# Attention into a mixture of experts on one core: products of zeros among the first heads, their stages skewed by one, and a third weight slot

## The chip, the cores and the metric

One core of a Trainium2 chip (trn2). The metric is device time in microseconds (us) of one execution, lower is better. The profile is of one such execution. Engines by the profile's names: PE (TensorE: matrix products and transposes, PEld its weight loads), DVE (VectorE), ACT (ScalarE), POOL (GpSimd), SP (the queue that issues all DMAs).

## The reference

```python
B, H, S, D = 4, 8, 576, 64          # attention
N, DM, E, FF = 2304, 512, 4, 1024   # experts, N = B * S
scores = q @ k^T / sqrt(D)
cum    = cumsum(log(clip(f, 1e-4, 1)))
scores = where(causal, -1e9, scores + cum_i - cum_j)
attn   = exp(scores - max) ; attn /= sum(attn) + 1e-9
x      = (attn @ v) with the heads side by side        # (2304, 512)
p      = probs / (sum(probs) + 1e-9)
out    = sum over e of p[:, e] * (relu(x @ w1[e]) @ w2[e])
```

All in float32.

## The kernel before, in words

**Tiles.** The tokens lie in 9 chunks of 256. A *job* is one batch, a pair of heads and a part of its queries (the first 256 or the other 320); a *head* in this text is one head of a job. Heads 0 to 7 (jobs 0 to 3, `FIRST = 8`) make the rows of chunk 0. A product of float32 operands is made of several in a reduced format: each operand is split into a high part (an ACT copy) and a low part (a subtraction on DVE or POOL).

**A head of the startup.** `prep_hi` copies the high part of q and k on ACT (`hi`, L297) and casts q on POOL (`q`, L298); `prep_lo` makes the low parts on POOL (`kl` L306, `hi` L312; on DVE for job 0). `qk_pe` makes the scores on PE (L350, four products), `qk_min` adds the mask and takes the maximum on DVE (L364), `qk_exp` is the exponential on ACT (L379, two tiles), `tr_pe` transposes on PE (L445, three), `tr_hi` (ACT, L455) and `tr_lo` (DVE, L462) split the transposed tile, `av_both` makes six products with v on PE (L493). After two heads `recip` (DVE L395 and L398, then POOL L400) and `spread` (a PE transpose L410 and an ACT copy L416) give the divisor, and `fin` multiplies on DVE (`xs`, L556) and splits into `xh` (ACT, L565) and `xl` (DVE, L568). `prep_v` splits v of a job (POOL L273, DVE L274). `late_sums` makes the second part of the running sums on DVE (L161) and sends them through DRAM for the later heads.

**Experts.** A *step* takes two weights (128 x 1024 each, the slices of w1 and w2 for 128 hidden units) for one chunk. Its first layer is `l1_k` (L698, 24 products of 256 columns: k = 0 to 3 is the pair of heads, so k needs `xh` of job k), then `gate` (ACT L709, DVE L710), then the second layer (L728, 12 products of 512 columns). `w_load` fetches a weight (512 KB) into a `wr` slot (SP, L644). `w_split` makes `wh` on ACT (L653) and `wl` in two halves (L657), on DVE for even weights below 16 and on POOL for all others. A `wr` slot is free when its split has ended. The first 8 steps use 16 weights once each.

**Order.** `startup()` writes the order of each engine by hand, stage by stage: in stage s head s has its exponential, head s+1 its scores, head s+2 its `prep`, head s-2 its products with v. Each engine runs its list in order. After it, a planner lays the steps and the heads from 8 on (`head_steps`, each with a due place through `pace`) on the engines. In that part PE always has first-layer and second-layer products in its list between those of the heads.

Of the kernel before, what the change touches and what calls it, by code (L numbers as in the profile page):

```python
# [29 lines left out]
DIRECT = (0, 1, 2, 3, 4)  # L30
LEAD = 3
W_DVE = tuple(range(0, 16, 2))
W_SLOT = (4, 5)
NEAR = 2
LATE = 6
L1_SLOT = {8: (0, 1), 9: (2,), 10: (3,)}
JOBS = ((0, 0), (1, 0), (2, 0), (3, 0), (0, 1), (1, 1), (2, 1), (3, 1))


# [32 lines left out]
def fused(ctx: ExitStack, tc: tile.TileContext, qk, v, f, probs, w, out):  # L72
# [13 lines left out]
    xh_p = SB("xh", 4)  # L86
    xf_p = SB("xf", 4)
    w_p = SB("w", 6)
    wr_p = SB("wr", 2)
    g_p = SB("g", 2)  # L90
    acc_p = SB("acc", 4)
    dr_p = ctx.enter_context(tc.tile_pool(name="dr", bufs=4, space=bass.MemoryType.DRAM))
# [20 lines left out]
    def decays():  # L113
        nc.sync.dma_start(out=fr, in_=f)
        first_loads()
        for t in q2:
            nc.gpsimd.memset(t[64:66, :].bitcast(F32), 8.0)
        make_identity(nc, ident)
        for t in [zero] + v4:
            nc.gpsimd.memset(t.bitcast(F32), 0.0)  # L120
        nc.vector.memset(ones, 1.0)
        for c in PARTS:
            nc.vector.tensor_scalar(
                out=fr[:, c], in0=fr[:, c], scalar1=1e-4, scalar2=1.0, op0=ALU.max, op1=ALU.min
            )
            nc.scalar.activation(out=fr[:, c], in_=fr[:, c], func=AF.Ln)
        nc.scalar.activation(out=warm, in_=ones[:, :1], func=AF.Exp)
        sums(0)
        nc.gpsimd.memset(mask, 0.0)
        nc.gpsimd.affine_select(  # L130
            out=mask[:, S - 128 :],
            in_=mask[:, S - 128 :],
            pattern=[[-1, 128]],
            compare_op=ALU.is_ge,
            fill=NEG,
            base=0,
            channel_multiplier=1,
        )
        for h in range(NEAR):
            jobs[0].near(h)  # L140
        for n in range(2):
            nc.sync.dma_start(out=ncd[:, n, :CH], in_=nc2[n][:, :CH].bitcast(F32))
        first_raw(2)
        for j in (0, 2):
            n = 1 if j == 0 else 0
            nc.sync.dma_start(
                out=first_kl[j // 2][64:66, 512 * n :].bitcast(F32).rearrange(
                    "p (h s) -> p h s", s=CH
                ),
                in_=ncd[2 * (j + n) : 2 * (j + 2), :, :CH].rearrange("h n s -> n h s"),  # L150
            )
        first_raw(3)
        w_load(0)
        w_load(1)
        nc.sync.dma_start(out=pr_r, in_=probs)
        jobs[NPR].load()

# [65 lines left out]
    class Job:  # L223
# [76 lines left out]
        def prep_lo(self, hh):  # L300
            if hh not in self.kl:
                self.rows(hh)
            wq, wk, ko, qo = self.wq, self.wk, self.ko, self.qo
            r, hi, kl = self.raw[:, hh, :], self.hi[hh], self.kl[hh]
            eng = nc.gpsimd if self.half == 0 and self is not jobs[0] else nc.vector
            eng.tensor_tensor(  # L306
                out=kl[:64, :wk],
                in0=r[:64, ko : ko + wk],
                in1=hi[:64, ko : ko + wk].bitcast(F32),
                op=ALU.subtract,  # L310
            )
            eng.tensor_tensor(  # L312
                out=hi[64:128, qo : qo + wq],
                in0=r[64:128, qo : qo + wq],
                in1=hi[64:128, qo : qo + wq].bitcast(F32),
                op=ALU.subtract,
            )

# [224 lines left out]
        def av(self, hh):  # L543
            self.av_pe(hh)
            self.av_top(hh)
            self.av_add(hh)

        def fin(self):
            w_ = self.wq
            pieces = place(self.b, self.half)  # L550
            k = self.pr
            direct = any(p[1] in DIRECT for p in pieces)
            if self not in jobs[:NPR]:
                self.spread()
            if direct:
                nc.vector.tensor_tensor(  # L556
                    out=self.xs[:, :w_],
                    in0=self.o[:, :w_] if self in jobs[:NPR] else self.xs[:, :w_],
                    in1=self.r[:, :w_],
                    op=ALU.mult,  # L560
                )
# [79 lines left out]
    def w_load(n):  # L641
        if n < NW and n not in wraw:
            wraw[n] = wr_p.tile([128, 1024], F32, tag="wr", name=f"wr{n}")
            nc.sync.dma_start(out=wraw[n], in_=w[n % 32])  # L644

    def w_split(n):
        if n >= NW:
            return
        w_load(n)
        wh[n] = w_p.tile([128, 1024], F32R, tag="wh", name=f"wh{n}")  # L650
        wl[n] = w_p.tile([128, 1024], F32R, tag="wl", name=f"wl{n}")
        r = wraw.pop(n)
        nc.scalar.activation(out=wh[n], in_=r, func=AF.Copy)  # L653
        for a in (0, 512):
            z = a + 512
            eng = nc.vector if n in W_DVE else nc.gpsimd
            eng.tensor_tensor(  # L657
                out=wl[n][:, a:z], in0=r[:, a:z], in1=wh[n][:, a:z].bitcast(F32), op=ALU.subtract
            )
        w_load(n + 1)  # L660
        w_load(n + 2)

    acc = {}
    l2 = {}
# [140 lines left out]
    def pace(n):  # L805
# [8 lines left out]
            m += 1  # L814
        upto(m)

    def startup():

        J = lambda h: heads[h] if 0 <= h < FIRST else (None, None)
# [4 lines left out]
        heads[0][0].prep_v()  # L824
        for h in range(2):
            J(h)[0].begin(h)
        heads[0][0].qk_pe(0, (0, 1))
        heads[0][0].qk_min(0, 0)
        heads[0][0].qk_min(0, 1)
        for s in range(FIRST + 3):  # L830
            (j, hh), (m, mm), (n, nn), (i, ii) = J(s), J(s + 1), J(s + 2), J(s - 2)
            if n:
                n.begin(nn)
                n.prep_hi(nn)
                n.prep_lo(nn)
            if m:
                m.qk_pe(mm, m.its)
                for t in m.its:
                    m.qk_min(mm, t)
            if j:  # L840
                for t in j.its:
                    j.qk_exp(hh, t)
            if i:
                i.av_both(ii)
            if j:
                j.tr_pe(hh, 0)
                j.tr_hi(hh, 0)
                j.tr_lo(hh, 0)
                if hh == 1:
                    j.recip()  # L850
                if hh == 0 and s > 0:
                    j.prep_v()
            if s >= 2 and s % 2 == 0 and s <= FIRST:
                heads[s - 1][0].spread()
            if s >= 4 and s % 2 == 0:
                heads[s - 4][0].fin()
            if s == LATE:
                late_sums()
            if s in W_SLOT:
                w_split(W_SLOT.index(s))  # L860
            for k in L1_SLOT.get(s, ()):
                if k == 0:
                    steps[0].l1_zero()
                for fi in range(2):
                    steps[0].l1_k(fi, k)
        j = heads[FIRST][0]
        w_split(2)
        j.prep(0)
        w_split(3)
        j.prep_v()  # L870
        j.begin(0)
        normalize()
# [1 line left out]
            w_split(n)  # L874

    pt0 = [pt_p.tile([128, 1216], F32R, tag=x, name=f"{x}_first") for x in ("pth", "ptl")]
    with tc.manual_schedule():
        startup()
    prev = None
# [66 lines left out]
```

## Time and profile before

| | |
|---|---|
| median of 3 runs | 1033.07 us (1031.91 to 1033.54) |
| the profiled execution | 1033.34 us, of which 1031.6 us are the span from the first to the last instruction |
| PE busy | 1003.7 us (97%) |
| DVE, ACT, POOL busy | 535.8, 447.5, 326.9 us |
| the chain that ended last | PE 88%, DMA 3%, DVE 3%, ACT 1%, POOL 1% |

How to read it: the chain is followed back from the last instruction to what released each one. The busy share of PE is counted in time, so a product that runs at half clock counts double; the granted clock has its own line.

### The profile page before, as it was taken

What the parts mean: (1) busy time and instruction counts of PE and PEld (TensorE: products, weight loads), DVE (VectorE), ACT (ScalarE), POOL (GpSimd) and SP (SyncE); (2) the same over time, 40 slices, a digit from 0 to 9 for tenths busy, and PEclk for the clock granted to TensorE, in tenths of its full rate; (3) what the DMA queues carried; (4) which work ended last, traced back from release to release, by engine and by line L of the source; (5) the groups of instructions that cost most, each with busy time, mean ns of one, the idle gap of its engine ahead of it and who ended that gap; (6) DMA issues with size and microseconds to landing.
All of it is one profiled execution on the core that took longest, in us unless ns stands there. A gap on an engine that the chain in (4) does not pass through costs nothing.

```text
span 1031.6 us, 16826 instructions
## 1 busy us (share of the span) xinstructions
PE 1003.7 (97%) x6561; PEld 917.3 (89%) x6561; DVE 535.8 (52%) x1181; ACT 447.5 (43%) x897; POOL 326.9 (32%) x357
## 2 busy tenths in 40 slices
PE   4789999999999999999999999999999999999998
PEld 4679899989999999999999999999999999999997
DVE  5667655686867756667566665532222222222222
ACT  5466765566656536455455455422121211212110
POOL 6466876251402204031223144213030311303010
PEclk9699999999999999999999999999999999999999
DMA  5255653342412314022131332211120202102001
GB/s 175 62 183 170 179 151 112 95 160 90 131 50 81 101 49 131 15 91 97 58 123 55 111 118 61 86 59 44 40 82 1 83 19 64 51 32 82 1 21 62
DMA packets 30544, 87.02 MB, mean 84 GB/s; under 512 B 3301, under 2 KB 5537, under 8 KB 30465
## 3 DMA queue, kind: packets, MB, share of 16 engines
q1 hardware_dynamic: 30464, 85.94, 26.5%
q8 instruction: 52, 0.85, 0.3%
q14 instruction: 28, 0.22, 0.1%
HBM read 81.06 MB, written 4.87 MB: 83 GB/s over the span
## 4 chain that ended last, share of the span: by engine, by line
PE 88%; DMA 3%; DVE 3%; ACT 1%; POOL 1%; issue 1%; SPq 0%; ACTq 0%; DVEq 0%; POOLq 0%
PE l L698 37%; PE l L728 36%; PE s L350 5%; PE t L445 5%; PE o L514 4%; DMA wr<-in_w 2%; DMA raw<-in_qk 1%; DVE wl L657 1%; ACT wh L653 1%; PE b L410 1%; POOL wl L657 0%; DVE v L285 0%; DVE hi L312 0%; POOL hi L312 0%; DVE xs L556 0%
## 5 line engine op out<-in xcount | busy, mean ns | idle before, releaser
L657 POOL TENSOR_TENSOR wl<-wr,wh 128x512 fp32r<-128x512 f32 x176 | 228.2, 1325 | 351.9 <-ACT wh L653 348.1
L698 PE MATMUL l<-xh,wh 128*128 128x256 f32 x1152 | 330.6, 287 | 3.1 <-ACT wh L653 3.0
L698 PE MATMUL l<-xh,wl 128*128 128x256 f32 x1152 | 327.9, 285 | 0.7 <-DVE wl L657 0.6
L698 PE MATMUL l<-xl,wh 128*128 128x256 f32 x1152 | 327.9, 285 | 0.1
L710 DVE SCALAR_TENSOR_TENSOR gl<-l,gh 128x512 fp32r<-128x512 f32 x144 | 99.1, 689 | 271.5 <-ACT gh L709 270.7
L728 PE MATMUL l<-wh,gh 128*128 128x512 f32 x576 | 231.1, 401 | 0.0
L698 PEld LDWEIGHTS l<-xh,wh 128*128 128x128 f32 x1152 | 220.8, 192 | 9.2 <-ACT wh L653 4.2
L728 PE MATMUL l<-wl,gh 128*128 128x512 f32 x576 | 227.5, 395 | 0.0
L698 PEld LDWEIGHTS l<-xl,wh 128*128 128x128 f32 x1152 | 220.7, 192 | 5.6 <-DVE xl L568 0.3
L728 PE MATMUL l<-wh,gl 128*128 128x512 f32 x576 | 225.5, 394 | 0.0
L698 PEld LDWEIGHTS l<-xh,wl 128*128 128x128 f32 x1152 | 220.6, 192 | 2.0 <-DVE wl L657 1.1
L709 ACT ACTIVATE gh<-l 128x512 fp32r<-128x512 f32 x144 | 85.5, 595 | 278.5 <-PE l L698 277.5
L379 ACT ACTIVATE p<-p,nm 128x576 f32<-128x576 f32 (+2 forms) x160 | 96.0, 601 | 92.1 <-DVE nm L364 91.7
L653 ACT ACTIVATE wh<-wr 128x1024 fp32r<-128x1024 f32 x96 | 100.0, 1054 | 68.1 <-DMA wr<-in_w 44.7
L728 PEld LDWEIGHTS l<-wh,gl 128*128 128x128 f32 x576 | 108.3, 188 | 23.0 <-DVE gl L710 0.4
L728 PEld LDWEIGHTS l<-wh,gh 128*128 128x128 f32 x576 | 109.1, 189 | 16.2 <-ACT gh L709 0.4
L728 PEld LDWEIGHTS l<-wl,gh 128*128 128x128 f32 x576 | 109.1, 189 | 15.5
L750 DVE SCALAR_TENSOR_TENSOR acc<-l,prob,acc 128x512 f32<-128x512 f32 x126 | 93.9, 748 | 28.8 <-PE l L728 26.1
L364 DVE CUSTOM_DVE_ANT_0 p<-s,mask 128x288 f32<-128x288 f32 (+2 forms) x160 | 75.9, 478 | 52.4 <-PE s L350 51.4
L298 POOL CAST q<-raw 64x320 fp32r<-64x320 f32 (+1 forms) x56 | 27.7, 496 | 226.7 <-PE s L350 208.9
L462 DVE TENSOR_TENSOR ptl<-t,pth 128x320 fp32r<-128x320 f32 (+2 forms) x120 | 65.9, 553 | 63.2 <-ACT pth L455 62.7
L445 PE MATMUL t<-ident,p 128*128 128x128 f32 x480 | 81.5, 279 | 4.0 <-ACT p L379 3.5
(80 smaller groups left out, 1001.5 us busy)
## 6 DMA issues: line engine op xcount, KB each, us to landing
wr<-in_w SPq DMA_DIRECT2D x96, 512.0 KB
raw<-in_qk SPq DMA_DIRECT2D x16, 896.0 KB
raw<-in_qk SPq DMA_DIRECT2D x12, 512.0 KB
vr<-in_v SPq DMA_DIRECT2D x16, 320.0 KB
out<-acc SPq DMA_DIRECT2D x16, 256.0 KB
first<-in_qk SPq DMA_DIRECT2D x4, 512.0 KB
vr<-in_v SPq DMA_DIRECT2D x12, 128.0 KB
first<-in_v SPq DMA_DIRECT2D x1, 512.0 KB
```

Source lines behind the costliest of these rows:

```text
L350: nc.tensor.matmul(out=ps[:, at : at + z - a], lhsT=lhsT, rhs=rhs, start=(m == 0), stop=(m == 1),)
L364: nc.vector.tensor_tensor_reduce(out=pt[:, a:z], in0=ps, in1=mask[:, m0 + a : m0 + z], scale=-0.125, scalar=BIG if n == 0 else nm[:, col : ...
L379: nc.scalar.activation(out=pt[:, :w_], in_=pt[:, :w_], func=AF.Exp, scale=-1.0, bias=self.nmax[hh][:, c : c + 1], accum_out=self.ssum[:, h ...
L445: nc.tensor.transpose(ps[:, at : at + 128], self.p[hh, it][:, TOK0[jt] : TOK0[jt] + 128], ident)
L462: nc.vector.tensor_tensor(out=lo[:, a0 + first : a0 + at - first], in0=ps[:, 2 * first : at], in1=hi[:, a0 + first : a0 + at - first].bitc ...
L653: nc.scalar.activation(out=wh[n], in_=r, func=AF.Copy)
L657: eng.tensor_tensor(out=wl[n][:, a:z], in0=r[:, a:z], in1=wh[n][:, a:z].bitcast(F32), op=ALU.subtract)
L698: nc.tensor.matmul(out=self.l1p[:, fi, :], lhsT=lhsT, rhs=rhs[:, k, :], start=(k == 0 and m == 0 and not self.whole), stop=(k == 3 and m = ...
L709: nc.scalar.activation(out=self.gh, in_=self.l1p, func=AF.Relu)
L710: nc.vector.scalar_tensor_tensor(out=self.gl, in0=self.l1p, scalar=0.0, in1=self.gh.bitcast(F32), op0=ALU.max, op1=ALU.subtract,)
L728: nc.tensor.matmul(out=l2[tt], lhsT=lhsT, rhs=rhs, start=(self.ps == 0 and fi == 0 and m == 0), stop=(self.ps == 1 and fi == 1 and m == 2),)
L750: nc.vector.scalar_tensor_tensor(out=acc[c][:, tt, :], in0=l2[tt], scalar=sc, in1=acc[c][:, tt, :], op0=ALU.mult, op1=ALU.add,)
```

## The change

- `idle_pe(n)` issues n products of the tile `zero` (128 x 128 by 128 x 512) into a PSUM tile that nobody reads: 8 before the first scores, one ahead of the transposes and one behind them in each stage with a head, 3 in each stage from 7 on (33 in all).
- The stages are skewed: `av_both` of a head stands one stage after its exponential (before: two), so there are 10 stages and not 11. The scores stand behind the last products with v of the stage before; the exponential stands ahead of the `prep` on ACT. `fin` of a job is cut in three calls (`fin_mult`, `fin_hi`, `fin_lo`) that stand in the odd stages from 3 on, two heads after the exponential of the job's second head. `prep_v` moves to the odd stages, behind `recip`.
- `prep_lo` makes the low part of q first, that of k second.
- Weight 0 is still split in stage 4, weight 1 in stage 6 (before: 5). `late_sums` moves from stage 6 to stage 8, with the split of weight 2 behind it (before: after the last stage). The split of weight 3 goes ahead of the `prep` of head 8.
- Step 0's first layer moves to stages 7 to 9 (before: 8 to 10).
- `wr` has three slots; weight 2 is fetched at the start, and a split of weight n fetches up to weight n+3.

```diff
-W_SLOT = (4, 5)
+W_SLOT = (4, 6)
-LATE = 6
-L1_SLOT = {8: (0, 1), 9: (2,), 10: (3,)}
+L1_SLOT = {7: (0, 1), 8: (2,), 9: (3,)}
-    wr_p = SB("wr", 2)
+    wr_p = SB("wr", 3)
             eng.tensor_tensor(
+                out=hi[64:128, qo : qo + wq],
...
+            )
+            eng.tensor_tensor(
                 out=kl[:64, :wk],
...
+        def fin_mult(self):
+            w_ = self.wq
+            nc.vector.tensor_tensor(
+                out=self.xs[:, :w_], in0=self.o[:, :w_], in1=self.r[:, :w_], op=ALU.mult
+            )
+        def fin_hi(self):
+            th, _ = x_tiles(self.b)
+            nc.scalar.activation(out=th[:, self.pr, :], in_=self.xs[:, :CH], func=AF.Copy)
+        def fin_lo(self):
+            th, tl = x_tiles(self.b)
+            nc.vector.tensor_tensor(
+                out=tl[:, self.pr, :],
+                in0=self.xs[:, :CH],
+                in1=th[:, self.pr, :].bitcast(F32),
+                op=ALU.subtract,
+            )
...
         w_load(1)
+        w_load(2)
...
+        w_load(n + 3)
...
+    def idle_pe(n):
+        for _ in range(n):
+            nc.tensor.matmul(out=idle_ps, lhsT=zero[:, :128], rhs=zero, start=True, stop=True)
+        idle_pe(8)
         heads[0][0].qk_pe(0, (0, 1))
...
-        for s in range(FIRST + 3):
+        for s in range(FIRST + 2):
+            (i, ii), (j, hh), (m, mm), (n, nn) = J(s - 1), J(s), J(s + 1), J(s + 2)
+            ends = s % 2 == 1
+            if ends and s >= 3:
+                heads[s - 2][0].fin_mult()
+            if j:
+                for t in j.its:
+                    j.qk_exp(hh, t)
+            if ends and s >= 3:
+                heads[s - 2][0].fin_hi()
             if n:
                 n.begin(nn)
-                n.prep_hi(nn)
-                n.prep_lo(nn)
+                n.prep(nn)
             if m:
                 m.qk_pe(mm, m.its)
                 for t in m.its:
                     m.qk_min(mm, t)
+            if ends and s >= 3:
+                heads[s - 2][0].fin_lo()
             if j:
+                idle_pe(1)
+                j.tr_pe(hh, 0)
+                idle_pe(1)
+                j.tr_hi(hh, 0)
+                j.tr_lo(hh, 0)
             if i:
                 i.av_both(ii)
+            if ends and j:
+                j.recip()
+                if m:
+                    m.prep_v()
+            if not ends and s >= 2:
+                i.spread()
             if s in W_SLOT:
                 w_split(W_SLOT.index(s))
+            if s >= FIRST - 1:
+                idle_pe(3)
             for k in L1_SLOT.get(s, ()):
...
+            if s == FIRST:
+                late_sums()
+                w_split(2)
         j = heads[FIRST][0]
-        w_split(2)
+        w_split(3)
         j.prep(0)
-        w_split(3)
         j.prep_v()
```

## Rows read from the trace of the kernel before

**Rows 1.** The page's span in 40 slices: busy tenths of PE, and the granted clock of PE in tenths.

```profile
PE   4789999999999999999999999999999999999998
PEclk9699999999999999999999999999999999999999
```

**Rows 2.** Busy time of the engines by stretch: the stretch in us, its length, PE busy (count), PEld, DVE, ACT, POOL, then the granted clock of PE, the DMA share and GB/s.

```profile
35.50:39.00 3.50, 1.41 (x9) 1.08 (x9) 2.82 (x8) 1.78 (x6) 0.33 (x2) 0.99 0.50 150
39.00:45.50 6.50, 5.15 (x23) 5.06 (x24) 1.79 (x7) 0.69 (x2) 0.74 (x2) 0.50 0.06 14
47.30:60.00 12.70, 12.53 (x80) 10.86 (x79) 10.44 (x26) 9.18 (x22) 9.00 (x10) 1.00 0.58 187
60.00:70.00 10.00, 9.28 (x60) 7.84 (x59) 6.34 (x13) 5.93 (x12) 7.00 (x9) 1.00 0.52 158
70.00:80.00 10.00, 7.66 (x46) 6.90 (x45) 7.46 (x19) 7.31 (x19) 6.77 (x9) 0.83 0.50 159
100.00:110.00 10.00, 9.38 (x62) 8.24 (x61) 6.52 (x18) 7.55 (x19) 9.43 (x10) 1.00 0.56 158
200.00:400.00 200.00, 199.50 (x1350) 184.14 (x1349) 146.94 (x342) 117.61 (x239) 53.29 (x59) 1.00 0.29 94
```

**Rows 3.** What PE waited for in the whole span: total us, times, longest us.

```profile
PE t L445 <- ACT p L379: 3.5, 3, 1.9
PE s L350 <- POOL hi L312: 3.3, 4, 1.1
PE l L698 <- ACT wh L653: 3.0, 2, 2.3
PE s L350 <- DMA kl<-ncd: 1.7, 1, 1.7
PE b L410 <- POOL rb L400: 1.4, 1, 1.4
PE o L514 <- DVE ptl L462: 0.6, 1, 0.6
PE l L698 <- DVE wl L657: 0.6, 1, 0.6
```

**Rows 4.** The longest wait of any engine between 45 and 130 us: total us, times, longest us.

```profile
ACT wh L653 <- DMA wr<-in_w: 12.9, 10, 2.9
```

**Rows 5.** Pieces of the chain that ended last, between 46 and 75 us: start, length, what.

```profile
46.01 1.05 ACT wh L653
...
49.00 3.63 DMA wr<-in_w
...
55.10 5.26 DMA wr<-in_w
...
73.67 1.06 ACT wh L653
74.78 0.50 PE l L698 x2
```

**Rows 6.** Instructions of ACT in the startup, in order of time: start, length, what, in brackets the idle time before it and its releaser. 17.07 is the exponential of head 2, 19.91 of head 3, 36.87 of head 7; 41.13 is the divisor's copy of job 3, 45.69 the `xh` of job 3.

```profile
17.07 0.39 ACT L379 ACTIVATE p<-p,nm 128x128 f32<-128x128 f32 x1
...
19.91 0.40 ACT L379 ACTIVATE p<-p,nm 128x128 f32<-128x128 f32 x1
...
28.21 0.61 ACT L297 ACTIVATE hi<-first 128x512 fp32r<-128x512 f32 x1
28.73 0.39 ACT L379 ACTIVATE p<-p,nm 128x128 f32<-128x128 f32 x1
...
36.54 0.42 ACT L565 ACTIVATE xh<-xs 128x256 fp32r<-128x256 f32 x1 [1.81 <-DVE xs L556]
36.87 0.39 ACT L379 ACTIVATE p<-p,nm 128x128 f32<-128x128 f32 x1
...
38.42 0.49 ACT L455 ACTIVATE pth_first<-t 128x384 fp32r<-128x384 f32 x1 [0.59 <-PE t L445]
41.13 0.38 ACT L416 ACTIVATE r<-b 128x256 f32<-128x256 f32 x1 [2.22 <-PE b L410]
...
45.69 0.42 ACT L565 ACTIVATE xh<-xs 128x256 fp32r<-128x256 f32 x1 [3.87 <-DVE xs L556]
```

**Rows 7.** Products on PE in the startup, as above. The first waits for rows of `kl` from DRAM; the next two have one shape; 40.69 is the only product of zeros of the kernel before; 47.20 is the last of step 0's first layer.

```profile
14.47 0.47 PE L350 MATMUL s<-kl,q 66*128 66x128 f32 x1 [1.67 <-DMA kl<-ncd]
...
16.77 0.41 PE L493 MATMUL o<-pth_first,v 128*128 128x256 f32 x1
...
20.52 0.28 PE L493 MATMUL o<-pth_first,v 128*128 128x256 f32 x1
...
40.69 0.78 PE L681 MATMUL l<-zero 128*128 128x512 f32 x1
...
47.20 0.28 PE L698 MATMUL l<-xh,wl 128*128 128x256 f32 x1
```

**Rows 8.** The low parts of a weight on DVE (two pairs) and on POOL (weight 3), and the low part of head 8's k on POOL, as above.

```profile
28.33 1.84 DVE L657 TENSOR_TENSOR wl<-wr,wh 128x512 fp32r<-128x512 f32 x2 [0.52 <-ACT wh L653]
...
47.66 0.73 POOL L306 TENSOR_TENSOR kl<-raw,hi 64x256 fp32r<-64x256 f32 x1 [7.02 <-ACT hi L297]
...
49.61 2.68 POOL L657 TENSOR_TENSOR wl<-wr,wh 128x512 fp32r<-128x512 f32 x2
...
53.75 1.29 DVE L657 TENSOR_TENSOR wl<-wr,wh 128x512 fp32r<-128x512 f32 x2 [0.68 <-ACT wh L653]
```

More of the change, by code (lines that the diff above doesn't have):

```diff
@@ L306, in prep_lo @@
             eng.tensor_tensor(
+                out=hi[64:128, qo : qo + wq],
+                in0=r[64:128, qo : qo + wq],
+                in1=hi[64:128, qo : qo + wq].bitcast(F32),
+                op=ALU.subtract,
+            )
+            eng.tensor_tensor(
                 out=kl[:64, :wk],
@@ L309, in prep_lo @@
                 in1=hi[:64, ko : ko + wk].bitcast(F32),
[L310 to L315, printed above, removed]
                 op=ALU.subtract,
@@ L546, in av @@
             self.av_add(hh)
+        def fin_mult(self):
[12 more added lines that the diff above has]
+                in1=th[:, self.pr, :].bitcast(F32),
+                op=ALU.subtract,
+            )
         def fin(self):
@@ L552, in fin @@
             direct = any(p[1] in DIRECT for p in pieces)
-            if self not in jobs[:NPR]:
-                self.spread()
+            self.spread()
             if direct:
@@ L557, in fin @@
                     out=self.xs[:, :w_],
-                    in0=self.o[:, :w_] if self in jobs[:NPR] else self.xs[:, :w_],
+                    in0=self.xs[:, :w_],
                     in1=self.r[:, :w_],
@@ L829, in startup @@
         heads[0][0].qk_min(0, 1)
-        for s in range(FIRST + 3):
-            (j, hh), (m, mm), (n, nn), (i, ii) = J(s), J(s + 1), J(s + 2), J(s - 2)
+        for s in range(FIRST + 2):
[8 more added lines that the diff above has]
+                heads[s - 2][0].fin_hi()
             if n:
                 n.begin(nn)
-                n.prep_hi(nn)
-                n.prep_lo(nn)
+                n.prep(nn)
             if m:
@@ L839, in startup @@
                     m.qk_min(mm, t)
+            if ends and s >= 3:
+                heads[s - 2][0].fin_lo()
             if j:
-                for t in j.its:
-                    j.qk_exp(hh, t)
+                idle_pe(1)
[3 more added lines that the diff above has]
+                j.tr_lo(hh, 0)
             if i:
                 i.av_both(ii)
[L845 to L858, printed above, removed]
+            if ends and j:
[4 more added lines that the diff above has]
+                i.spread()
             if s in W_SLOT:
                 w_split(W_SLOT.index(s))
+            if s >= FIRST - 1:
+                idle_pe(3)
             for k in L1_SLOT.get(s, ()):
@@ L876, in fused @@
     pt0 = [pt_p.tile([128, 1216], F32R, tag=x, name=f"{x}_first") for x in ("pth", "ptl")]
+    idle_ps = ps_1.tile([128, 512], F32, tag="l1", name="idle")
     with tc.manual_schedule():
```

## The prediction

> **What bounds the kernel now.** I read the slices first: PE is full from about 47 us on and its clock sags only in the second slice [rows 1]. Then the stretches: from 200 us on PE is busy 99.8% at full clock [rows 2], and neither the products nor their order there are changed. What can move is what PE loses before. Its waits name it [rows 3]: in the startup the exponentials, POOL's low parts, the rows of `kl` from DRAM and POOL's divisor; after it the high and low parts of weights. Next to the waits stands the clock: it was at half from 39 to 45.5, after a stretch in which PE had worked 1.41 of 3.5 us [rows 2]. Before 25 us the clock column reads 1.00, but a product of 256 columns lasted 0.41 us at 16.77 and 0.28 at 20.52 [rows 7], so I take the clock there from durations: half at first, full from between these two. Last the chain: between 46 and 75 us it goes from a split to the transfer into its slot, to the next split, to PE [rows 5], and ACT waited 12.9 us for weights in 10 waits [rows 4]. Two pieces therefore set the end: when step 0's first layer is through (47.20 + 0.12 = 47.3 us [rows 7]; I call this X) and what PE loses behind it.
>
> **The weights: third slot.** The even weights 2 to 10, five of them, began their splits at 46.01 and, the last, at 73.67 [rows 5]: 27.7 us for four pairs, 6.9 us a pair with two slots. One round of a slot is a transfer of 3.6 to 5.3 us [rows 5], ACT's 1.05 and 1.3 us of DVE or 2.7 of POOL [rows 8], so a pair costs 6.0 to 9.0. With three slots the same round carries three weights: 4.6 us a pair. PE needs for a step 24 x 256 + 12 x 512 columns, 5.1 us at 2.4 GHz, and the heads' products come on top. So weights stop being last. What was lost to them: 3.0 + 0.6 us of PE's waits [rows 3], and the half clock after the longest (2.3 us): 0.17 of the 10 us from 70 to 80 [rows 2], 1.7 us. Sum 5.3. The waits of 0.6 for `ptl` stay. The first weights come in time too: weight 4 is asked for when POOL ends with weight 1, near 38.5, and lands by 42.5 to 44 (before: 52.6, the end of the transfer from 49.00). Bounds: 3.6 if the clock sags all the same, 5.9 if the 0.6 for `ptl` goes as well.
>
> **The stages up to the exponential of head 7 (before: 36.87 [rows 6]).** Head 2's scores wait for DRAM rows until 14.47 [rows 7], a transfer that is not moved, so its exponential stays at about 16.9. After that I add up what follows what. Exponential to the high part of the transposed tile is 36.87 to 38.42, 1.55 us [rows 6]. In an even stage PE then has a zero product (512 columns: 0.21 us at 2.4 GHz, 0.43 at 1.2), six products with v (1152 columns, 0.48 or 0.96) and the divisor's transposes (0.2 or 0.4, 0.3 until ACT sees them), and ACT's copy (0.3) stands ahead of the next exponential: 3.05 us at full clock, 4.2 at half. An odd stage is ACT's own work: exponentials 0.9, `xh` 0.42, `hi` 0.61, high part 0.49 [rows 6], 2.15 with the overlaps. Stages 4 and 6 carry a weight's high part on ACT (0.95 to the next start). In stage 5 `fin_mult` stands on DVE behind weight 0's low parts, 1.84 us [rows 8], and ACT's `xh` and head 7's `hi` behind it: 1.5 more. So head 3 at 16.9 + 3.7 = 20.6 (before 19.91), head 4 at 22.75, 5 at 26.75, 6 at 30.4, 7 at 34.4 with full clock, 36.7 with half in stages 4 and 6. I take 35.6: 1.3 us won. The skew itself wins a stage; the zeros and the copy ahead of the exponential give most of it back. The cover of the zeros is the wait for exponentials; where it is gone they cost 16 x 0.21 or 16 x 0.43, and this is the difference of the bounds. The eight at the start run from 2.5 us on, done by 6, before the first scores at 8.8: nothing.
>
> **From there to X.** Exponential to high part 1.55; then on PE a zero product, head 6 with v, three zeros, step 0's zero product, 12 first-layer products, head 7 with v, the transposes: 3.9 us at full clock, 7.4 at half. The divisor's copy thus starts 5.3 to 9.0 after the exponential; I take 7.2, since the clock was half in this place before [rows 2]: 42.8 (before 41.13 [rows 6]). Now weight 2's split stands ahead of the last `fin`: on ACT 0.3 + 1.05, on DVE 1.3 to 1.84 (`fin_mult` is queued behind it, and `late_sums` has ended by then), then `xs` 0.41, `xh` 0.42 and 0.25 of hand-overs: 3.9. Six products with the wait for `xl`: 1.1. X is 47.8, 0.5 later than before. PE waits some 2.0 us in this place (42.8 + three zeros, six products, three zeros = 44.7, against 46.7). Waits of 1.9 and 2.3 us were followed by half clock [rows 2, 3, 5], shorter ones of 1.1 were not always; half a chance of the 1.7 us seen at 70 to 80 is 0.9. Startup: 1.4 us lost. Bounds: 2.8 won (full clock all through, X = 44.5) to 4.2 + 1.7 lost (half clock all through, X = 51.5).
>
> The low parts of a pair on DVE lasted 1.84 us beside POOL's subtractions and 1.29 elsewhere [rows 8]. The Trainium skill (SBUF — State Buffer, Summary: rules for kernel authors) says that of a DVE instruction with two SBUF inputs and a GpSimd one that reads SBUF the second to issue blocks until the first has ended; by that the pair in stage 4 would cost 1.29 + 2 x 0.73 = 2.75, as an estimate, and the sum would be 0.9 higher. The row shows a delay of this kind but smaller, and the sum uses the row.
>
> **The sum.** 1033.34 + 1.4 - 5.3 = 1029.4; the profiled execution stands 0.27 above the median, so I write 1029.4 for the median too. Under 0.2% (2.1 us) a measurement of this kernel hardly tells from no change.
>
> **Rivals.** (a) The zeros hold the clock at full through the startup: X = 44.5 and no sag behind it, 1033.3 - 2.8 - 5.3 = 1025.2. For it: the zeros fill part of the waits that stood between PE's bursts. Against it: stages 4 to 6 still hold waits for DVE and POOL of over 1 us, and stage 9 one of 2. The Trainium skill (TensorE: Matmul & The Clock Gate, Why this matters for your kernels) advises dense work to leave half clock and no idle gaps to stay out of it; that rule would give this case, and the drop after 39 us agrees with its second half.
> (b) The zeros run at half clock and PE sets the stages: X = 51.5, the sag behind it, 1033.3 + 5.9 - 5.3 = 1033.9, no change. For it: half clock from 39 to 45.5 under continuous work. Against it: the same work brought the clock back at 45.5.
> (c) Slower: weight 3's low part on POOL (2.7 us [rows 8]) now stands ahead of head 8's `hi` and `kl` (before `kl` started at 47.66, ahead of it). If the heads of chunk 1, not the weights, are what ends last before step 16, all of them come 2.7 us later and the weights' 5.3 are not seen: 1033.3 + 1.4 + 2.7 = 1037.4. For it: POOL busy 9.43 of 10 us from 100 to 110 [rows 2] and the 0.6 for `ptl`. Against it: the chain of [rows 5], and those heads' ACT work stood behind the 12.9 us of waits [rows 4]. It decides once more than 4 us of PE waits stand at heads between 80 and 115.
> (d) The third slot does nothing, because transfers share the engines or the planner lays the splits as before: 1033.3 + 1.4 = 1034.7. Against it: a DMA share of 0.5 to 0.6 [rows 2].
>
> **How the numbers follow.** Forecast 0.46 (its own range 1027 to 1032), (a) 0.17, (b) 0.14, (c) 0.13, (d) 0.10. The range 1025.0 to 1035.0 holds the forecast, most of (a), (b) and (d); left out are (c) and a little below. Faster: 0.40 of the forecast, 0.17 of (a), 0.01: 0.58. Slower: (c) 0.13 and edges of (b) and (d) 0.04: 0.17. The rest, 0.25, within the bound.
>
> **What would show it.** Right: no wait of PE for `wh` or `wl` above 0.5 us after X, ACT's wait for weights down from 12.9 to under 4, full clock from 60 us on; X between 46 and 50; a wait of PE near 2 us for `xh` of job 3, with DVE's `xs` behind `wl`. Wrong: X at 45 or less (a), at 51 or more (b), waits at `ptl`, `hi` or `p` near 110 (c), weight transfers still last (d).

## The result and the profile after: 0.9% slower

The changed kernel takes 1042.06 us (1040.48 to 1042.71) against 1032.49 (1031.81 to 1033.54) for the kernel before on the same chip: ratio 1.009, 95% interval 1.0072 to 1.0107. The profiled execution has a span of 1040.9 us, against 1031.6 before. Line numbers below are those of the changed kernel, which has moved most lines by 18 to 20: the first layer is L717, the second L747, the gate L728 (ACT) and L729 (DVE), `w_split` L671 and L675, `fin_mult` L550, `fin_hi` L556.

The page of after, the span in 40 slices (PE's busy tenths, its granted clock in tenths):

```profile
PE   6889999999998999999999999999999999999998
PEclk8899999999999999999999999999999999999999
```

Beside [rows 1] the first slices are a little better filled, and one slice that was full before no longer is: the thirteenth, 312 to 338 us. The stretches of after show it more closely; the columns are those of [rows 2].

```profile
39.00:45.50 6.50, 6.50 (x41) 6.05 (x40) 2.39 (x6) 1.67 (x3) 1.87 (x2) 0.83 0.33 94
...
50.00:60.00 10.00, 7.60 (x35) 6.15 (x36) 9.80 (x14) 5.55 (x9) 8.00 (x10) 0.83 0.45 128
60.00:70.00 10.00, 9.27 (x66) 8.49 (x65) 5.15 (x14) 5.88 (x15) 6.89 (x9) 1.00 0.71 231
70.00:80.00 10.00, 10.00 (x66) 9.01 (x65) 8.13 (x13) 6.04 (x15) 6.74 (x8) 1.00 0.62 196
80.00:100.00 20.00, 18.43 (x125) 16.27 (x123) 15.75 (x36) 13.54 (x30) 11.74 (x13) 1.00 0.54 172
...
110.00:130.00 20.00, 17.67 (x118) 15.49 (x118) 16.74 (x38) 11.50 (x30) 14.72 (x19) 1.00 0.47 149
130.00:200.00 70.00, 70.00 (x484) 64.68 (x483) 40.53 (x113) 42.96 (x108) 41.08 (x52) 1.00 0.39 113
...
310.00:320.00 10.00, 9.49 (x65) 8.38 (x64) 8.27 (x24) 4.97 (x12) 0.99 (x3) 1.00 0.28 93
320.00:330.00 10.00, 7.61 (x43) 6.52 (x43) 8.68 (x23) 7.82 (x18) 1.09 (x3) 0.83 0.13 35
```

The 10 us from 70 to 80 went from 7.66 busy at a clock of 0.83 [rows 2] to 10.00 at 1.00: the third slot did that. From 310 to 330 PE lost 2.9 us and then clock, where before it was busy throughout:

```profile
310.00:320.00 10.00, 10.00 (x72) 9.34 (x71) 8.51 (x21) 6.01 (x15) 0.85 (x2) 1.00 0.11 33
320.00:330.00 10.00, 10.00 (x72) 9.29 (x71) 6.35 (x19) 7.24 (x15) 3.00 (x4) 1.00 0.28 95
```

What PE waited for in after, first from 44 to 130 us, then from 130 us to the end (total us, times, longest):

```profile
PE l L747 <- DVE gl L729: 3.6, 2, 2.3
PE o L514 <- DVE xs L574: 1.4, 3, 0.6
...
PE l L717 <- POOL wl L675: 0.6, 1, 0.6
...
PE t L445 <- ACT p L379: 1.2, 1, 1.2
PE t L445 <- DVE xs L574: 0.7, 1, 0.7
PE s L350 <- DVE ptl L462: 0.6, 2, 0.4
PE t L445 <- DVE nm L364: 0.5, 1, 0.5
```

The weights of [rows 3] have left the list but for 0.6. In their place stands the low part of a gate, and late in the span waits at operands of heads, all between 316 and 325 us; before, that whole part held one wait of 0.5.

Where the 9.3 us of span come from can be counted. I added up the products of both traces by their columns at full clock, zeros left out (good to about 1 us: it depends on what a transpose and the gap between two products are counted at), and compared how much of the same work each kernel had done at a given time:

| PE work done beside before, us | at 50 | 60 | 80 | 130 | 310 | 330 |
|---|---|---|---|---|---|---|
| after | -0.3 | -4.1 | +0.8 | -3.0 | -3.2 | -8.8 |

So: nothing in the startup, 3.8 lost from 50 to 60, 4.9 won from 60 to 80, 3.8 lost from 80 to 130, 5.6 lost from 310 to 330, and nothing from there on.

**The place at 310 to 330.** The gates of the expert steps on ACT say what is waited for; first before, then after (start, length, in brackets the idle time before):

```profile
305.25 0.60 ACT L709 ACTIVATE gh<-l 128x512 fp32r<-128x512 f32 x1
318.50 0.60 ACT L709 ACTIVATE gh<-l 128x512 fp32r<-128x512 f32 x1 [0.80 <-PE l L698]
```

```profile
303.55 0.58 ACT L728 ACTIVATE gh<-l 128x512 fp32r<-128x512 f32 x1
...
329.88 0.60 ACT L728 ACTIVATE gh<-l 128x512 fp32r<-128x512 f32 x1 [0.51 <-PE l L717]
```

These are the gates of step 33 and step 34. Step 33 comes 1.7 us sooner than before, step 34 11.4 later. Step 34 is the first for chunk 4, which needs the 32 heads 8 to 39 behind the startup (jobs 4 to 19). The reciprocal of job 19, its last, on DVE, in before and then in after:

```profile
300.59 0.18 DVE L398 RECIPROCAL rs<-ss 128x6 f32<-128x6 f32 x1
```

```profile
315.67 0.17 DVE L398 RECIPROCAL rs<-ss 128x6 f32<-128x6 f32 x1
```

It is 15.1 us late. In the order of products on PE, head 39's first scores stand behind 31.0 steps' worth of expert products (counted by columns) in the kernel before and behind 33.1 in after: the steps run two further ahead of the heads, and then nothing is left to lie between the heads' own waits.

**The place at 50 to 60.** PE in after, the last product of step 0's first layer, the wait, the scores of head 8 (which stood at 49.59 before):

```profile
48.77 0.28 PE L717 MATMUL l<-xh,wl 128*128 128x256 f32 x1
...
55.05 0.79 PE L747 MATMUL l<-wh,gl 128*128 128x512 f32 x1 [2.30 <-DVE gl L729]
...
59.66 0.39 PE L350 MATMUL s<-hi 128*128 128x128 f32 x2
```

The same time on DVE, and POOL's low parts of weights 3 and 5:

```profile
49.38 2.12 DVE L285 TENSOR_TENSOR v<-vr,v 128x128 fp32r<-128x128 f32 x2 [1.24 <-ACT v L284]
...
52.58 1.81 DVE L675 TENSOR_TENSOR wl<-wr,wh 128x512 fp32r<-128x512 f32 x2
54.31 1.27 DVE L729 SCALAR_TENSOR_TENSOR gl<-l,gh 128x512 fp32r<-128x512 f32 x2
55.51 3.09 DVE L285 TENSOR_TENSOR v<-vr,v 128x128 fp32r<-128x128 f32 x2
...
48.76 2.59 POOL L675 TENSOR_TENSOR wl<-wr,wh 128x512 fp32r<-128x512 f32 x2 [7.53 <-ACT wh L671]
...
55.74 2.51 POOL L675 TENSOR_TENSOR wl<-wr,wh 128x512 fp32r<-128x512 f32 x2
```

Two pairs of splits of v, small instructions, end when POOL's pair ends (51.50 beside 51.35, 58.60 beside 58.25). DVE's list is thereby late, and the gate's low part, ready to start at 51.5 (its `gh` on ACT began at 50.92), starts at 54.31. Of the two pairs only the first stands ahead of it: some 1.6 us more than the 0.48 of a pair in before, to which weight 4's low part adds 0.5 (1.81 beside 1.29 [rows 8]). Grouped by line from 44 to 130 us, first before, then after, then with POOL's two weights moved to DVE (run h3 below):

```profile
L285 DVE TENSOR_TENSOR v<-vr,v 128x128 fp32r<-128x128 f32 x14 | 6.1, 476 | 0.2
```

```profile
L285 DVE TENSOR_TENSOR v<-vr,v 128x128 fp32r<-128x128 f32 x12 | 14.1, 1212 | 1.4 <-ACT v L284 1.2
```

```profile
L285 DVE TENSOR_TENSOR v<-vr,v 128x128 fp32r<-128x128 f32 x12 | 8.8, 757 | 0.1
```

One split of v lasts 1212 ns on average in after and 476 in before.

### The profile page after: what moved, and what is told of

It reads as the page before. It is cut to its first block, busy times and chain, and to the rows that moved or that the text cites. A ratio compares the mean times of both kernels' runs of the same rounds, so it can differ in the third digit from the quotient of the medians.

```text
span 1040.9 us, 16905 instructions
## 1 busy us (share of the span) xinstructions
PE 1014.1 (97%) x6594; PEld 922.3 (89%) x6594; DVE 543.1 (52%) x1181; ACT 447.7 (43%) x897; POOL 322.1 (31%) x357
## 4 chain that ended last, share of the span: by engine, by line
PE 88%; DVE 4%; ACT 3%; DMA 2%; issue 2%; POOL 1%; SPq 0%; ACTq 0%; DVEq 0%
PE l L717 37%; PE l L747 36%; PE s L350 5%; PE t L445 5%; PE o L514 4%; ACT wh L671 1%; DVE v L285 1%; DMA wr<-in_w 1%; PE b L410 1%; ACT hi L297 1%; DVE ss L395 1%; DVE wl L675 1%; PE o L493 1%; DMA raw<-in_qk 0%; DVE acc L769 0%
## 5 line engine op out<-in xcount | busy, mean ns | idle before, releaser
L675 POOL TENSOR_TENSOR wl<-wr,wh 128x512 fp32r<-128x512 f32 x176 | 225.8, 1313 | 361.7 <-ACT wh L671 345.5
L717 PE MATMUL l<-xh,wh 128*128 128x256 f32 x1152 | 329.1, 287 | 0.2
L717 PE MATMUL l<-xh,wl 128*128 128x256 f32 x1152 | 326.2, 283 | 0.6 <-POOL wl L675 0.6
L717 PE MATMUL l<-xl,wh 128*128 128x256 f32 x1152 | 326.6, 284 | 0.0
L729 DVE SCALAR_TENSOR_TENSOR gl<-l,gh 128x512 fp32r<-128x512 f32 x144 | 99.1, 689 | 274.4 <-ACT gh L728 273.7
L747 PE MATMUL l<-wh,gh 128*128 128x512 f32 x576 | 231.1, 401 | 0.0
L747 PE MATMUL l<-wh,gl 128*128 128x512 f32 x576 | 227.1, 395 | 3.6 <-DVE gl L729 3.6
L747 PE MATMUL l<-wl,gh 128*128 128x512 f32 x576 | 227.6, 395 | 0.0
L717 PEld LDWEIGHTS l<-xh,wh 128*128 128x128 f32 x1152 | 219.6, 191 | 6.1 <-issue 0.6
L717 PEld LDWEIGHTS l<-xl,wh 128*128 128x128 f32 x1152 | 219.8, 191 | 5.4 <-DVE xl L560 0.2
L717 PEld LDWEIGHTS l<-xh,wl 128*128 128x128 f32 x1152 | 219.5, 191 | 1.2 <-POOL wl L675 0.8
L728 ACT ACTIVATE gh<-l 128x512 fp32r<-128x512 f32 x144 | 85.8, 595 | 289.6 <-PE l L717 288.9
L747 PEld LDWEIGHTS l<-wh,gl 128*128 128x128 f32 x576 | 108.8, 189 | 27.2 <-DVE gl L729 4.5
L747 PEld LDWEIGHTS l<-wh,gh 128*128 128x128 f32 x576 | 109.1, 189 | 16.1 <-ACT gh L728 0.2
L747 PEld LDWEIGHTS l<-wl,gh 128*128 128x128 f32 x576 | 109.2, 189 | 15.5
L671 ACT ACTIVATE wh<-wr 128x1024 fp32r<-128x1024 f32 x96 | 98.7, 1051 | 46.3 <-PE l L747 35.9
```

What stands on the lines that cost most here:

```text
L675: eng.tensor_tensor(out=wl[n][:, a:z], in0=r[:, a:z], in1=wh[n][:, a:z].bitcast(F32), op=ALU.subtract)
L717: nc.tensor.matmul(out=self.l1p[:, fi, :], lhsT=lhsT, rhs=rhs[:, k, :], start=(k == 0 and m == 0 and not self.whole), stop=(k == 3 and m = ...
L728: nc.scalar.activation(out=self.gh, in_=self.l1p, func=AF.Relu)
L729: nc.vector.scalar_tensor_tensor(out=self.gl, in0=self.l1p, scalar=0.0, in1=self.gh.bitcast(F32), op0=ALU.max, op1=ALU.subtract,)
L747: nc.tensor.matmul(out=l2[tt], lhsT=lhsT, rhs=rhs, start=(self.ps == 0 and fi == 0 and m == 0), stop=(self.ps == 1 and fi == 1 and m == 2),)
```

## The experiments

### Each half alone: three slots, and the startup without them

e1 is the kernel before with the third slot only; e2 is the changed kernel with two slots.

```diff
-    wr_p = SB("wr", 2)
+    wr_p = SB("wr", 3)
...
+        w_load(2)
...
+        w_load(n + 3)
```

These are the lines of e1; e2 has them the other way round.

> The kernel before with the third weight slot alone (slot, weight 2 fetched at the start, weights up to n+3 fetched by a split). Theory S (with weights early the planner runs the expert steps ahead of the heads, so that PE has none left to fill the heads' waits in front of step 34): PE's waits for weights between 45 and 130 us are gone (-5), but waits of PE at heads appear between 300 and 330 us, and the sum is 1030 to 1036 us. Theory O (the order of the startup makes the heads late, the slot does what was forecast): 1026 to 1030 us, no waits of PE at heads after 130 us. Theory Z (the zero products): as O.

> The changed kernel with two weight slots. Theory S: weights are late again (waits of PE for weights between 50 and 110 us), the stretch from 300 to 330 us loses less than 3 of its 5.5 us; 1035 to 1041 us. Theory O: as the changed kernel plus the weights' waits, 1042 to 1047 us, with the waits from 300 to 330 us as they are. Theory Z: 1042 us or more.

Measured: e1 1.0051 (1.0034 to 1.0067), e2 1.0071 (1.0052 to 1.009). Both halves lose. e1, at 1038.38 us above the range of every theory, has the signs of theory S: from 310 us on

```profile
310.00:320.00 10.00, 6.83 (x42) 4.92 (x40) 7.98 (x23) 7.46 (x18) 1.19 (x3) 1.00 0.29 93
```

and the reciprocal of job 19 stands at 310.55, 10.0 late. By counted work e1 was some 2 us ahead of before at 310 and 3.5 behind at 330. The slot wins something, less than the 5.3 forecast, and more than that is lost when chunk 4 is due. Its heads are late although nothing of the startup's order was touched: the steps' weights come sooner, the planner lays 2.1 steps more ahead of the same heads, and a step is some 5.1 us of products.

e2 came to 1039.39 us, in the range of S, but not with its sign. Without the third slot ACT waited 11.3 us for weights again, and still the steps ran 1.9 further ahead of head 39, job 19's reciprocal came 10.6 us late (311.18) and some 4 us of counted work were lost from 310 to 330, where S had less than 3. So the steps get ahead of the heads in two ways, by the slot alone and by the new startup alone.

### The order at the end of the startup, and the zeros

e3 prepares head 8 ahead of the split of weight 3 again; e4 leaves out the 33 products of zeros.

```diff
-        w_split(3)
         j.prep(0)
+        w_split(3)
...
-        for _ in range(n):
+        for _ in range(0):
```

> The changed kernel with the operands of head 8 ahead of the split of weight 3, as before. Theory O: the 2.3 us wait for gl near 55 us and the clock's sag behind it go, the heads stand where they stood, 1032 to 1037 us. Theory S: the wait near 55 goes or shrinks, but the waits from 300 to 330 us stay, 1037 to 1042 us. Theory Z: within 2 us of 1042.

> The changed kernel without the 33 products of zeros (the one that opens step 0's first layer stays). Theory Z: 1030 to 1037 us. Theories S and O: step 0's first layer ends within 2 us of 47.2, everything behind it is as in the changed kernel, 1040 to 1044 us.

Measured: e3 1.0127 (1.0107 to 1.0147), 1045.15 us, slower still and outside all three ranges; e4 1.0086 (1.0062 to 1.0109), 1041.91 us, no different from after, though its four times lie from 1038.6 to 1043.8 and the trace is of the fastest. Theory O, in the form that head 8's place behind weight 3 makes the heads late, fell: with head 8 first PE waits longer for the same gate,

```profile
PE l L747 <- DVE gl L729: 5.4, 2, 4.3
```

and a pair of splits of v lasted 3.35 us there. It isn't the place of one preparation; in this trace too DVE's list is late. The zeros are not the cause of the loss either, nor of the better clock from 39 to 45.5 us: it was 0.79 there in e4 and 0.83 in after.

### Holding the heads on purpose

By then one relation ran through the profiled executions: the end is late by the delay of job 19 less about 6 us. g1 tests it in the kernel before, with heads delayed by work that nobody reads (and by weight 3's split, which stands ahead of them).

```diff
-        j.prep(0)
         w_split(3)
+        slow = x_p.tile([128, 320], F32, tag="xs", name="slow")
+        nc.gpsimd.memset(slow, 0.0)
+        for _ in range(12):
+            nc.gpsimd.tensor_tensor(out=slow, in0=slow, in1=slow, op=ALU.add)
+        nc.gpsimd.tensor_copy(out=q2[0][:64, :], in_=slow[:64, :])
+        j.prep(0)
```

> The kernel before; at the end of the startup weight 3's split goes ahead of the preparation of head 8, and POOL does a memset, 12 additions of 128x320 and a small copy (work that nobody reads) between the two. Nothing else is changed: two slots, no zeros, no skew. Theory H (the 32 heads of the first four chunks are a chain that has to be through before step 34, and the kernel before has only some 5.6 us to spare in it): the reciprocals of jobs 7 to 19 come 8 to 14 us later than before, and the run ends at this delay less 5 to 6 us, so 1035 to 1042, with the loss as PE waits and half clock between 300 and 335 us; the gates of the steps up to 33 are no later by as much. Rival P (what is lost is what PE loses before 130 us; the later wait moves with it by chance): the steps fill PE while the heads are held, PE loses 1 to 2 us before 130, and the run ends within 1031 to 1034 with nothing at 300 to 335.

Measured: 1.0119 (1.01 to 1.0137), 1045.49 us. The delay came out larger than I expected (18.8 us), and the time with it; PE lost 1.8 us from 320 to 330, and the relation held:

| profiled execution | job 19's reciprocal, us after before's | span, us after before's | difference |
|---|---|---|---|
| after | 15.1 | 9.3 | 5.8 |
| e1 | 10.0 | 3.8 | 6.2 |
| e2 | 10.6 | 5.0 | 5.6 |
| e3 | 18.2 | 12.4 | 5.8 |
| e4 | 11.5 | 5.2 | 6.3 |
| g1 | 18.8 | 12.9 | 5.9 |

The kernel before had some 6 us to spare at step 34; what the heads are late beyond that is lost in full. This by itself doesn't say that step 34 is the place (g1 lost 8 of its 12 us of counted work ahead of 130 us), which the later runs do. Nor does it hold for every kernel: in g2 and g3, below, job 19 was 7.0 and 4.7 us late and the span 5.6 and 4.2 us longer, lost elsewhere.

### Heads 8 and 9 begun inside the startup

g2 takes them into the skew of the changed kernel, g3 and g4 into the order of before with two and with three slots. The lines of g4 beside e1 (g3 has the same beside before, g2 the same heads at the same stages of its own order):

```diff
-LATE = 6
+LATE = 3
+        X = lambda h: heads[h] if 0 <= h < FIRST + 2 else (None, None)
...
+            if s in (8, 9):
+                e, ee = X(s)
+                e.qk_pe(ee, e.its)
...
+                    e.qk_min(ee, t)
...
+                    e.qk_exp(ee, t)
...
+            if s in (6, 7):
+                e, ee = X(s + 2)
+                e.begin(ee)
+                e.prep(ee)
```

> The changed kernel, in which heads 8 and 9 follow the same skew as heads 0 to 7 (prepared in stages 6 and 7, scores in 7 and 8, exponentials in 8 and 9) and the row sums of late_sums move to stage 3; zeros and three slots stay. Theory H: the chain behind the startup starts two heads further on, jobs 10 to 19 come 8 to 12 us sooner than in the changed kernel (their delay against before falls from 14 to 17 us to 4 to 7), PE has no wait above 0.5 us at 300 to 335, and the time falls from 1042 to 1030 to 1035. Rival P: the two heads' work stands ahead of step 0's products, X comes 1 to 3 us later, and the time stays at 1040 to 1046.

> The kernel before with two slots, no zeros and its own order of the stages; only heads 8 and 9 are begun inside it (prepared at the end of stages 6 and 7, scores and exponentials in stages 8 and 9) and late_sums moves to stage 3. Theory H: more is to spare in the heads' chain than before uses, so nothing is won by that; X comes 0 to 2 us later and the waits for weights stay: 1031 to 1036. Rival (heads are what is last even before 130 us): 1027 to 1030.

> The same with the third weight slot, still without zeros and with the order of the stages of before. Alone the third slot gave 1038.4. Theory H: the slot let the steps run ahead and left the heads 10 us behind; with two heads begun early their delay is 0 to 5 us, no waits at 300 to 335 remain, and what the slot saves in waits for weights is seen: 1028 to 1033. Rival (the third slot costs by itself, by its transfers or its order on the engines): 1036 to 1041 as without the early heads.

Measured: g2 1.0064 (1.0048 to 1.0081), g3 1.0035 (1.0023 to 1.0047), g4 1.0007 (0.9997 to 1.0016). g4 gives back nearly all of e1's loss, its heads no longer late (job 19 at 0.0); the time is 1 us above the expected range. g2's heads came sooner than after's (job 11 by 6 us, job 19 by 8, of 8 to 12 expected) and PE was full from 300 to 340, as expected; yet the time missed by 4 us, since by counted work it had lost some 7 us at 60 already, in one wait:

```profile
PE o L514 <- DVE nm L364: 6.9, 1, 6.9
```

DVE stood in a single instruction there, the last of the normalization (72 columns), which lasted 0.47 us in after; POOL was at four halves of weights:

```profile
52.66 5.75 DVE L185 TENSOR_TENSOR prob<-pr_r,psum__115 128x72 f32<-128x72 f32 x1
```

```profile
53.40 4.92 POOL L676 TENSOR_TENSOR wl<-wr,wh 128x512 fp32r<-128x512 f32 x4
```

So there are two losses, and early heads only mend the later one. g3 starts from the kernel before, which does not have that later loss, and was slower (0.35%): early heads have a price of their own.

### Chunk 4 wanted two steps later

The direct test of the place: the same products, but the first sweep's last group also runs for chunk 3, so that chunk 4 is first needed by step 36 (and chunk 3 by step 28, before: 32).

```diff
-    ((0,), (0,), (0, 1), (0, 1, 2)),
-    ((1, 2, 3, 4), (1, 2, 3, 4), (2, 3, 4), (3, 4)),
+    ((0,),) * 4 + ((0, 1),) * 2 + ((0, 1, 2), (0, 1, 2, 3)),
+    ((1, 2, 3, 4),) * 4 + ((2, 3, 4),) * 2 + ((3, 4), (4,)),
...
-        for c in sets[g // 2]
+        for c in sets[g]
```

> The changed kernel; chunk 4 is first wanted by step 36 instead of step 34: in the first sweep the last group of two weights also runs for chunk 3, in the second sweep only for chunk 4 (the same products and weights in all; zeros, skew and three slots stay, and the planned order of TensorE is the same up to step 27). Theory H (the heads of chunk 4, 14 to 17 us later than before, are what step 34 waits for): the waits and the half clock of 315 to 328 go, and with them 4 to 6 us: 1036 to 1038. Rival P (the loss comes from what PE loses before 130 us and would show up at some place in any case): 1040 to 1043.

> The kernel before with the third slot (1038.4 alone) and with chunk 4 first wanted by step 36. Theory H: the slot wins 2.5 us up to 310 us, as the counted work of the run with the slot alone shows, and the 5.6 us lost behind it go: 1029 to 1032, faster than the kernel before. Rival P: 1036 to 1040.

> The kernel before with three slots and heads 8 and 9 begun inside the startup (1033.9 alone), and chunk 4 first wanted by step 36. Theory H: its heads were no longer behind (delay 0 at jobs 19 and 20) and it lost only 0.9 us at 310 to 320, so chunk 4's place is worth 0.5 to 2 us here: 1031.5 to 1033.5. If it wins 4 us or more, as the others are expected to, the later place is worth something apart from the heads' delay, and H is at least incomplete.

> The kernel before (two slots) with chunk 4 first wanted by step 36 and nothing else. Theory H: before had some 5.6 us to spare at step 34, so the later place changes nothing: 1031.5 to 1033.5. If it wins over 2 us, the place is worth something for another reason and what it gave the changed kernel is no measure of the heads' delay.

Measured: h1 1.0029 (1.0019 to 1.0039), 1036.03 us; h2 0.9979 (0.997 to 0.9989), 1030.93; h4 0.9994 (0.9985 to 1.0003), 1032.0; i1, the control, 0.9998 (0.9986 to 1.0009), 1032.38. All four as theory H had it. In h1 the heads are as late as in after (job 19 at +15.2), and it costs nothing there any more:

```profile
310.00:320.00 10.00, 10.00 (x68) 9.26 (x68) 7.61 (x19) 5.23 (x11) 0.95 (x2) 1.00 0.29 92
320.00:330.00 10.00, 10.00 (x64) 9.03 (x63) 7.33 (x19) 5.30 (x13) 0.88 (x2) 1.00 0.11 35
```

From 130 us to the end the profile lists no wait of PE in h1. Rival P fell: the loss at 310 to 330 is not one that shows up somewhere in any case. h1 is 6.0 us faster than after, h2 7.4 us faster than e1, and i1 no faster than before. With the place moved, the third slot alone (h2) is 0.2% faster than the kernel before, 2 us where the prediction had booked 5.3.

### POOL's low parts moved to DVE

h3 is h1 with the low parts of weights 3 and 5 on DVE.

```diff
-W_DVE = tuple(range(0, 16, 2))
+W_DVE = (0, 2, 3, 4, 5, 6, 8, 10, 12, 14)
```

> The first of these with the low parts of weights 3 and 5 on VectorE instead of GpSimd. In the changed kernel VectorE's two splits of v lasted 2.12 and 3.09 us beside GpSimd's low parts of these two weights and stood ahead of the gate that PE waited 2.3 us for. Theory (the 3.2 us still lost before 130 us come from VectorE held up by GpSimd): the pairs of v last under 1 us, the wait for the gate's low part falls under 0.7 us, and 2 to 4 us are won against the first: 1032 to 1036. Rival (VectorE has too much work in its list whoever does it: 2 x 1.29 us more): no difference of over 1 us, or a loss.

Measured: 0.9983 (0.9973 to 0.9993), 1031.25 us, 4.8 less than h1 and a little under the expected range. The mean of a split of v fell to 757 ns (above), the wait for the gate's low part from 3.4 in all to

```profile
PE l L747 <- DVE gl L729: 0.9, 1, 0.9
```

(0.7 was expected; of the pairs of v, expected under 1 us, the mean was 1.5), and by counted work h3 was 1.3 us behind before at 60, where h1 was 3.5. DVE had two more pairs to do and was still earlier. Some 2 us of the gain lie there, some 3.5 from 80 to 130. The two weights also leave POOL's list, on which the later heads' low parts stand; no run separates that from DVE's delay, so 4.8 us is the price of these two weights' place on POOL, and the trace shows one way in which it is paid.

### What is left of zeros and skew

i2 has the slot, the later chunk and the DVE low parts, but the startup of before, without zeros and skew (it is h2 with the low parts of weights 3 and 5 on DVE); i3 is h3 without its zeros; i4 is h3 with heads 8 and 9 in the skew.

> The kernel before with three slots, chunk 4 first wanted by step 36 and the low parts of weights 3 and 5 on VectorE; no zeros, no skew. Beside the same with zeros and skew (1031.25). Theory N (zeros and skew move the start by 0.1 us and are worth nothing): 1029.5 to 1032. Rival (they win the 1 us or more that the start was meant to win): 1032.5 to 1035. Rival (they cost): below 1029.5.

> The changed kernel with chunk 4 first wanted by step 36 and the low parts of weights 3 and 5 on VectorE, without its 33 products of zeros. Theory N: 1030 to 1032.5, as with them. If the zeros hold TensorE's clock to some use: 1033 or more.

> The changed kernel with heads 8 and 9 in the skew (1039.4 alone), chunk 4 first wanted by step 36 and the low parts of weights 3 and 5 on VectorE. With early heads alone it lost 7 us in one wait of 6.9 us at 53 us, with VectorE held up, and none at 300 to 335. Theory (GpSimd's low parts held VectorE up there): that wait falls under 3 us and the time to 1029 to 1034. Rival (the place of the early heads causes the wait): 1036 to 1040.

Measured: i2 0.9931 (0.9914 to 0.9948), 1025.72 us, the fastest of all and faster than both kernels. Theory N fell here: beside h3 (1031.25 us; each beside its own runs of the kernel before) the zeros and the skewed stages, with all that the change moves along with them, cost some 5 us even with the two main losses out of the way. Beside h2, i2 is a second test of the two weights' place, in the other startup: 0.9979 became 0.9931, again some 5 us. The stretches where the cost of zeros and skew shows, i2 first, then h3:

```profile
60.00:80.00 20.00, 19.79 (x140) 17.94 (x139) 17.31 (x39) 14.87 (x33) 16.25 (x19) 1.00 0.67 217
80.00:130.00 50.00, 50.00 (x346) 46.24 (x346) 33.05 (x82) 34.91 (x82) 38.62 (x43) 1.00 0.53 156
```

```profile
60.00:80.00 20.00, 18.97 (x124) 16.63 (x123) 16.22 (x27) 11.49 (x24) 13.74 (x16) 1.00 0.50 169
80.00:130.00 50.00, 47.95 (x322) 43.53 (x321) 34.20 (x81) 33.42 (x78) 34.95 (x42) 1.00 0.52 164
```

Which of the two costs it stays open: i3's times lay in two groups, four from 1028.1 to 1031.6 us and six from 1035.8 to 1037.3, and its ratio, 1.001 (0.9987 to 1.0033), decides nothing; its trace is of the fastest run and can't explain the others. i4 came to 1.0013 (1.0004 to 1.0022), 1033.81 us: g2's wait of 6.9 us is gone, as expected, with 4.6 us of waits for `xs` in another place.

## Why the prediction was wrong, step by step

| step | forecast, us | measured (counted PE work) |
|---|---|---|
| startup up to 50 us | 0.5 lost | 0.3 lost |
| the wait behind it and the half clock | 0.9 lost | 3.8 lost (50 to 60) |
| third slot: weights' waits and their clock | 5.3 won | 4.9 won (60 to 80) |
| 80 to 130 | 0 | 3.8 lost |
| behind 130 | 0 | 5.6 lost (310 to 330) |
| sum | 3.9 won | 8.6 lost (span: 9.3) |

**Right.** The third slot: ACT's wait for weights fell from 12.9 [rows 4] to

```profile
ACT wh L671 <- DMA wr<-in_w: 3.4, 3, 1.9
```

no wait for `wh` was left and one of 0.6 for `wl` (0.5 was allowed), and the clock was full from 60 to 80; rival (d) is out. Its size was not right: the 4.9 us won from 60 to 80 have the loss from 50 to 60 ahead of them. With the slot alone (e1) PE waited 1.5 us for a gate's low part there, and only some 2 us were left of the gain by 310 us; h2 won 2 us and not 5.3. X was 48.9, within its bounds (forecast 47.8, before 47.3). The wait of 2 us for `xh` of job 3 did not show on PE, since nine products of step 1 had been laid in it, so the later X cost nothing by itself. Rivals (a) and (b) are out as well: the clock from 39 to 45.5 was 0.83 on average, neither full nor half, and 0.79 without the zeros (e4).

**Off, with little effect.** The exponential of head 7 started at 37.10, 0.2 later than before [rows 6]; I had 35.6, and 36.7 as the late bound. What the skew won the zeros gave back: the reciprocal of job 3 stood at 40.10 in after, at 37.65 without the zeros (e4) and at 39.65 in before. The divisor's copy came at 44.23 and not at 42.8.

**The step that failed first** is the sentence "from 200 us on PE is busy 99.8% at full clock [rows 2], and neither the products nor their order there are changed". A PE that was busy at 310 in the kernel before did not have to stay busy: the heads of chunk 4 had some 6 us to spare there and no more. And the order did change: the planner laid two more steps ahead of the same heads, with the third slot alone (e1) and with the new startup alone (e2), and the steps used up what was to lie between the heads of chunk 4. How the planner came to that no run shows. The price is 5.6 us by counted work at 310 to 330; h1 (6.0 us) and h2 (7.4) give it back by moving the due place. Rival (c) held this mechanism, but with one place (step 16; chunk 1 is first wanted by step 10) and one cause (2.7 us of POOL) and a chance of 0.13. The heads were not 2.7 but 15 us late, some 1.5 us were lost around step 10 (110 to 130 us) and none from 130 to 310: what decided was the next due place with no filler ahead of it, step 34, and 6 us of slack.

**The second** is what I put behind X: "half a chance of the 1.7 us". PE did wait 2.30 us and went to half clock (0.50 from 55.0 to 58.2), but at the gate's low part and not at `xh`. I asked what the moved weight 3 does to POOL and to head 8, and not what POOL's pair does to DVE's list behind it: a pair of splits of v, the normalization, weight 4's low part, then the gate. The moved weight is not needed for it, since e1, where it was not moved, has a wait of 1.5 us at the same operand. The Trainium skill (SBUF — State Buffer, Summary: rules for kernel authors) says that of a DVE instruction with two SBUF inputs and a GpSimd instruction that reads SBUF the second to issue blocks until the first has ended; the trace of after agrees, with v pairs of 2.12 and 3.09 us that end with POOL's pairs, where the shortest pair lasted 0.48 in before. I had weighed that rule only for one pair of low parts, taken the milder row for it (1.84) [rows 8], and not carried it to the short instructions. Taking the two weights off POOL gave back 4.8 us (h3) and some 5 (i2 beside h2); how much of that is DVE's delay and how much POOL's shorter list stays open.

**The third** was not looked for: zeros, skew and what moves with them cost some 5 us beyond these two (i2 beside h3), from 60 to 130 us. I had the startup at 1.4 in all. That DVE's and POOL's lists there are laid on heads which stand differently is what the stretches suggest; no run splits it further. In after, part of what is lost there has the form of the second step. An addition to four columns lasted until POOL's pair of low parts (118.57 to 121.09) had ended, the gate's low part stood behind it, and PE, until 122.04, waited 1.34 us for that:

```profile
117.94 3.19 DVE L395 TENSOR_SCALAR ss<-ss 128x4 f32<-128x4 f32 x1 [1.20 <-ACT p L379]
```

In before the six of its kind from 40 to 130 us lasted 0.15 to 1.26.

## What to carry to other kernels

Where a planner lays one kind of work into the gaps of another, taking a limit from the one lets it run ahead of the other: look for the next place where the other is due and ask what will lie in its gaps then, however busy the engine looks there now. When work is moved on GpSimd, read VectorE's list of the same microseconds, the small instructions too: here several of them ended only when GpSimd's pair ended. A third buffer that looks like a loss alone (1.0051) won 0.2% once the due place was moved, and 0.7% with two low parts on another engine as well (what these two would be worth without the slot no run shows).

## What the runs showed of the hardware

A DVE instruction can wait for several POOL instructions in a row. In h3 POOL ran four halves of weights back to back, and a pair of DVE's halves that started meanwhile ended at 68.62, after all of them (67.27); such a pair lasted 1.29 us elsewhere [rows 8]. DVE first, then POOL:

```profile
62.96 5.66 DVE L675 TENSOR_TENSOR wl<-wr,wh 128x512 fp32r<-128x512 f32 x2
```

```profile
62.23 5.04 POOL L675 TENSOR_TENSOR wl<-wr,wh 128x512 fp32r<-128x512 f32 x4
```

The first of the pair took 4.86 of these 5.66 us. The 5.75 us of 72 columns in g2, above, are the same.
